# One transfer of an adaptive-norm transformer block's modulation matrix, split by partitions

## The chip, the cores and the metric

The kernel runs on one core of one Trainium2 chip. The metric is the device time of one execution in microseconds (us); lower is better. A core has five engines with instruction streams of their own: TensorE (PE: matmuls, with weight loads shown as PEld), VectorE (DVE), ScalarE (ACT), GpSimd (POOL) and SyncE (SP), which here issues DMA transfers only. The transfers of SP and ACT run on the core's 16 DMA engines.

## The reference

One transformer block over 2048 tokens of width 640, in bf16. A vector c gives six modulation vectors of 640, which scale, shift and gate two sub-blocks: attention with 32 heads of 20 over a causal window of 256 tokens, and a gated feed-forward of width 1536.

```python
mod = (silu(c) @ w_mod).reshape(1, 6, 1, -1)          # w_mod: 640 x 3840
sa, ca, ga, sb, cb, gb = (mod[:, i] for i in range(6))
h = layernorm(x) * (1 + ca) + sa
x = x + ga * attention(h, A_wqkv, A_wo)               # 0 <= query - key < 256
h = layernorm(x) * (1 + cb) + sb
x = x + gb * ((sigmoid(h @ w_gate) * (h @ w_up)) @ w_down)
```

## The kernel before

Tokens are worked in eight chunks of 256, each two blocks of 128 rows. A chunk goes through layer norm, transposes, the modulation, the q, k and v projections, windowed attention, the output projection, the second layer norm and the feed-forward; work of neighbouring chunks is interleaved.

The program is first written as a list of operations (`A(...)`, in the class `Prog`), each with its engines, what it reads and writes, and an assumed cost. The order in which they are issued is written out by hand in the list `PLAN` (L365): each code is five times an operation's number plus the number of its engine (0 TensorE, 1 ScalarE, 2 VectorE, 3 GpSimd, 4 SyncE). `emit` (L262) turns the dependencies into semaphore waits. Every engine works its instructions strictly in that order, so an instruction that waits holds up all behind it on its engine. Transfers take one of 24 semaphores in turn (`NDMA`, L25), and a transfer whose semaphore was used before waits for the transfer that used it.

The beginning is what the change touches. `load_bulk` (L621) loads a weight matrix in pieces of row blocks. For the first modulation matrix, `wm0` (the columns of w_mod for sa and ca, 640 x 1280), it makes five transfers, one for each block of 128 rows: 128 partitions of 2560 bytes, 320 KB (KiB). They go into the memory that later holds wd, so the profile names them wd<-in_w_mod_dram; all transfers show line L584. They are operations 18 to 22, and the plan has them on SP in the order of blocks 1, 0, 3, 2, 4 (codes 99, 94, 109, 104, 114). Ahead of them stand c, a part of wq (240 KB) and two blocks of x (160 KB each, one issued by SP, one by ACT); behind them on SP the rest of wq, two more blocks of x, and wk, wo and wv.

TensorE meanwhile runs matmuls on zeros (L679), then transposes the normalized first x block. For each block of wm0 it then has ten matmuls (`fnA`, L768) that add silu(c) times that block into the bank psA, with filling matmuls on zeros (L690) between some, and the transposes of the second x block between blocks 1 and 2. VectorE copies the sum into mA (L778); with mA, ScalarE, VectorE and GpSimd modulate the transposed x, hT (L831, L832), and the first projections (wq, hT) follow.

Of the kernel before, what the change touches and what calls it, by code (L numbers as in the profile page):

```python
# [360 lines left out]
def c_pe(n):  # L361
# [129 lines left out]
MW = 64  # L491
# [14 lines left out]
def build(nc, A_x, A_wqkv, A_wo, B_x, B_w_gate, B_w_up, B_w_down, c, w_mod, out, S=2048):  # L506
    NCH = S // CH
    P = Prog(nc)
    A = P.op
# [55 lines left out]
    def R(name):  # L565
        return Res(name)

    R_w3 = {k: [R(k + "0"), R(k + "1")] for k in ("wq", "wk", "wv")}
    R_crow, R_ident, R_ccol, R_cth, R_siluc, R_silubc = (R(n) for n in ("crow", "ident", "ccol", "cth", "siluc", "silubc"))
# [45 lines left out]
    Rm = [[R(f"wm{i}_{kt}") for kt in range(NDT)] for i in range(4)]  # L615
# [149 lines left out]
    oA = []  # L765
# [622 lines left out]
```

## Time and profile before

| | us |
|---|---|
| median of three runs | 324.57 |
| the three runs | 322.55, 324.57, 632.56 |
| the profiled execution, whole | 323.56 |
| its span, first to last instruction | 321.8 |
| TensorE busy in the span | 315.6 (98%) |

The profile is of one execution. A busy time sums what an engine's instructions cover; matmuls are pipelined and overlap, so a covered stretch need not be work at full speed. "L698 PE MATMUL S<-silubc,wd" is line, engine, operation, and the tile written and those read; "x10" is how many. A bracket such as [0.50 <-DVE x L815] gives the idle time of the engine ahead of the row, and what ended it. Rows of SPq and ACTq are transfers being issued; from issue to landing is told by another view. The chain of work that ended last is followed back from the last instruction to what released each. In the view by stages, each engine's busy time (and instructions) stands in the order PE, PEld, DVE, ACT, POOL, then TensorE's granted clock, the share in which the 16 DMA engines were busy, and GB/s.

### The profile page before, as it was taken

How to read it: one execution, taken by the hardware profiler on the slowest of the kernel's cores; microseconds unless marked ns; L12 is line 12 of the kernel's file. 1: busy time of each engine (PE TensorE's matmuls, PEld its weight loads, DVE VectorE, ACT ScalarE, POOL GpSimd, SP SyncE). 2: the span in 40 equal slices, each digit the busy share in tenths (PEclk: the TensorE clock that was granted, in tenths of full speed). 3: DMA queues.
4: the chain of work that ended last, by engine and by line, in shares of the span. 5: the costliest groups of instructions: out<-in, count | busy, mean ns of one | idle time of the engine just before them, and what ended most of it. 6: DMA issues, size and time to landing. Idle time of an engine off the chain costs nothing.

```text
span 321.8 us, 11465 instructions
## 1 busy us (share of the span) xinstructions
PE 315.6 (98%) x5045; PEld 236.8 (74%) x5045; DVE 198.8 (62%) x424; ACT 213.9 (66%) x229; POOL 189.5 (59%) x349
## 2 busy tenths in 40 slices
PE   6999999999999999999999999999999999999996
PEld 2677767677877777766777677877877777877885
DVE  4689987877886746584555555465534474386323
ACT  2699997877787986768686867676976746411220
POOL 3338759878768493949484848577575826601000
PEclk9999999999999999999999999999999999999999
DMA  7999999999922534126526100220800004002101
GB/s 249 348 262 278 223 179 248 194 225 295 206 36 43 88 75 55 44 63 108 77 19 111 37 22 2 63 42 25 132 18 4 22 22 104 20 5 61 43 0 41
DMA packets 62123, 32.92 MB, mean 102 GB/s; under 512 B 45946, under 2 KB 60794, under 8 KB 62074
## 3 DMA queue, kind: packets, MB, share of 16 engines
q1 hardware_dynamic: 59904, 29.73, 43.5%
q10 hardware_dynamic: 2170, 2.46, 2.8%
q8 instruction: 39, 0.64, 0.9%
q14 instruction: 10, 0.08, 0.1%
HBM read 18.68 MB, written 2.62 MB: 66 GB/s over the span
## 4 chain that ended last, share of the span: by engine, by line
PE 96%; DMA 1%; DVE 1%; ACT 1%; issue 0%; ACTq 0%
PE M L698 79%; PE S L699 8%; PE M L699 7%; DMA x<-in_A_x_dram 1%; ACT hT L831 1%; DVE st L793 1%; PE S L698 1%; PE S L690 0%; ACT stg L914 0%; ACTq L584 0%; DVE x L815 0%; DVE st L795 0%; ACT hT L914 0%; DVE x L1308 0%; DVE mA L778 0%
## 5 line engine op out<-in xcount | busy, mean ns | idle before, releaser
L1067 ACT ACTIVATE E<-S 128x2048 bf16<-128x2048 f32 x56 | 105.0, 1875 | 40.6 <-PE S L699 40.2
L1072 POOL TENSOR_SCALAR_AFFINE_SELECT E<-E 128x256 bf16<-128x256 bf16 x112 | 46.6, 427 | 57.1 <-ACT E L1067 25.1
L1076 POOL TENSOR_SCALAR_AFFINE_SELECT E<-E 128x512 bf16<-128x512 bf16 x112 | 70.6, 646 | 4.6 <-DVE x L815 1.2
L698 PE MATMUL M<-h2T,wg 128*128 128x256 bf16 x480 | 67.0, 273 | 0.0
L698 PE MATMUL M<-h2T,wu 128*128 128x256 bf16 x480 | 66.7, 273 | 0.0
L1289 DVE SCALAR_TENSOR_TENSOR hh<-sig,M 128x512 bf16<-128x512 f32 x48 | 32.4, 678 | 42.9 <-ACT sig L1287 26.4
L698 PE MATMUL M<-wd,hh 128*128 128x320 bf16 (+2 forms) x396 | 57.1, 295 | 0.0
L698 PEld LDWEIGHTS M<-h2T,wg 128*128 128x128 bf16 x480 | 45.4, 98 | 7.8 <-DVE T L1162 0.2
L698 PEld LDWEIGHTS M<-h2T,wu 128*128 128x128 bf16 x480 | 45.2, 98 | 7.3
L1287 ACT ACTIVATE sig<-M 128x512 f32<-128x512 f32 x48 | 28.5, 595 | 31.2 <-PE M L698 30.9
L698 PEld LDWEIGHTS M<-wd,hh 128*128 128x128 bf16 x396 | 37.2, 98 | 13.7 <-DVE hh L1289 0.2
L1045 POOL TENSOR_SCALAR_AFFINE_SELECT E<-E 128x1024 bf16<-128x1024 bf16 x28 | 32.0, 1147 | 4.9 <-ACT E L1041 3.4
L699 PEld LDWEIGHTS S<-QT,KT 20*64 20x64 bf16 (+1 forms) x1856 | 20.0, 100 | 17.4 <-issue 9.7
L699 PE MATMUL S<-QT,KT 20*64 20x256 bf16 (+5 forms) x1856 | 32.3, 228 | 0.4 <-issue 0.4
L1041 ACT ACTIVATE E<-S 128x2048 bf16<-128x2048 f32 x14 | 26.3, 1876 | 6.8 <-PE S L699 6.7
L793 DVE BATCH_NORM_STATS2 st<-x 128x6 f32<-128x320 bf16 x64 | 28.9, 479 | 2.4 <-DMA x<-in_A_x_dram 1.8
L1162 DVE STREAM_TRANSPOSE T<-M 128x512 f32<-128x512 f32 x32 | 21.5, 700 | 12.9 <-PE S L699 11.6
L698 PE MATMUL M<-wk,hT 128*128 128x320 bf16 x160 | 27.9, 299 | 0.0
L1308 DVE TENSOR_TENSOR x<-M,x 128x320 bf16<-128x320 f32 (+2 forms) x33 | 15.4, 475 | 18.8 <-PE M L698 18.6
L698 PE MATMUL M<-wq,hT 128*128 128x320 bf16 x160 | 26.2, 299 | 0.7 <-DVE hT L832 0.5
L698 PE MATMUL M<-wv,hT 128*128 128x320 bf16 x160 | 26.0, 299 | 0.0
L698 PE MATMUL M<-wo,oT 128*128 128x320 bf16 x160 | 25.9, 299 | 0.0
(84 smaller groups left out, 356.4 us busy)
## 6 DMA issues: line engine op xcount, KB each, us to landing
x<-in_A_x_dram SPq DMA_DIRECT2D x18, 160.0 KB, 3.7
wd<-in_w_mod_dram SPq DMA_DIRECT2D x6, 320.0 KB, 5.4
wd<-in_B_w_down_dram SPq DMA_DIRECT2D x4, 480.0 KB, 5.5
wu<-in_w_mod_dram SPq DMA_DIRECT2D x5, 320.0 KB, 4.8
x<-in_A_x_dram ACTq DMA_DIRECT2D x8, 160.0 KB, 2.7
out_dram<-x SPq DMA_DIRECT2D x8, 160.0 KB, 1.9
wu<-in_B_w_up_dram SPq DMA_DIRECT2D x2, 576.0 KB, 4.7
wg<-in_B_w_gate_dram SPq DMA_DIRECT2D x2, 576.0 KB, 6.8
```

The source lines that it names most:

```text
L698: return e.matmul(o, l, r, start=st, stop=sp, skip_group_check=True)
L699: return e.matmul(o, l, r, start=st, stop=sp, tile_position=tp, skip_group_check=True)
L793: A("dve", lambda e, g, bi=bi, j=j: e.bn_stats(v(bi * 12 + j * 6, 6), src[bi].ap[:, j * 320:(j + 1) * 320]), 0.48, reads=[src[bi].r()], wr ...
L1041: A("act", lambda e, eng: e.activation(cell().rearrange("p m (x c) -> p m x c", c=64)[:, :, 0:4:3, :], Sp.ap[:].rearrange("p j (k x c) -> ...
L1045: A("pool", lambda e, eng, c0=c0, pat=pat, base=base, cm=cm: e.affine_select(cell()[:, :, c0:c0 + 64], cell()[:, :, c0:c0 + 64], pattern=p ...
L1067: A("act", lambda e, eng: e.activation(part(0, 512), Sp.ap[:], ACT.Exp, scale=SM_SCALE), 1.876, reads=[Sp.r()], writes=[E.r("C"), E.r("B") ...
L1072: A("pool", lambda e, eng, hc=hc, src=src, far_h=far_h: e.affine_select(side(hc), part(src, 64), pattern=[[0, 4], [-1 if far_h else 1, 64] ...
L1076: A("pool", lambda e, eng, c0=c0, near=near: e.affine_select(part(c0, 128), part(c0, 128), pattern=[[0, 4], [1 if near else -1, 128]], com ...
L1162: A("dve", lambda e, g, h=h: e.transpose(T1.ap[:, 512 * h:512 * h + 512], X[h].ap), 0.694, reads=[X[h].r()], writes=[T1.r(h)], prio=3.5, t ...
L1287: A("act", lambda e, g, pg=pg, sg=sg: e.activation(sg.ap[:], pg.ap[:], ACT.Tanh, scale=0.5), c_act(512), reads=[pg.r()], writes=[sg.r()], ...
L1289: A("dve", lambda e, g, pu=pu, sg=sg, f0=f0: e.scalar_tensor_tensor(out=hh.ap[:, f0:f0 + 2, :], in0=sg.ap[:].rearrange("p (a b) -> p a b", ...
L1308: A("dve", lambda e, g, ps=ps, bi=bi, c0=c0, n=n: e.tensor_tensor(x1[bi].ap[:, c0:c0 + n], ps.ap[:, 0:n], x1[bi].ap[:, c0:c0 + n], op=ALU. ...
```

## The change

The transfer of block 0 of wm0 becomes two, one for partitions 0 to 119 and one for partitions 120 to 127. They are issued by SP one right behind the other, at the old one's place. The second has a result of its own, `R_wm0x`, and the ten matmuls of block 0 wait for both. Since there is one operation more, every operation from number 19 on has its number raised by one, and with it its code in the plan; apart from the added code 99 behind 94 the plan's order is the same.

```diff
 PLAN = [
-    119, 53, 76, 3, 8, 297, 86, 84, 300, 305, 333, 270, 277, 99, 281, 48, 442, 335, 28, 437, 447, 94, 13, 287, 422, 427,
...
+    124, 53, 76, 3, 8, 302, 86, 84, 305, 310, 338, 275, 282, 104, 286, 48, 447, 340, 28, 442, 452, 94, 99, 13, 292, 427,
...
     def load_bulk(dst, src, Rs, work, prio, tag, extra=(), cuts=(1, 2, 3, 4, 5), dlat=2.24):
         k = 0
         for m in cuts:
+            if tag == "wm0" and k == 0:
+                dma(lambda: dst[0:120, 0:1, :], lambda: src[0:120, 0:1, :], 0.8, writes=Rs[0:1], prio=prio, tag=tag, dlat=dlat, tmin=0.44, lat=0.18)
+                dma(lambda: dst[120:128, 0:1, :], lambda: src[120:128, 0:1, :], 0.08, writes=[R_wm0x], prio=prio, tag=tag, dlat=dlat, tmin=0.44, lat=0.18)
+                k = m
+                continue
...
+    R_wm0x = R("wm0x")
     load_bulk(wm_ap[0], wm_src[:, :, 0:1280], Rm[0], 0.88, 0.2, "wm0", dlat=2.89)
...
-        oA.append(A("pe", fnA, MW / 2400.0 * 10, reads=[Rm[0][kt], R_silubc], writes=[psA.r()], prio=0, lat=0.2, tag="modA"))
+        oA.append(A("pe", fnA, MW / 2400.0 * 10, reads=[Rm[0][kt], R_silubc] + ([R_wm0x] if kt == 0 else []), writes=[psA.r()], prio=0, lat=0.2, tag="modA"))
```

218 rows, old and new, of the table PLAN are left out of this document.

## The prediction

> **What bounds the kernel now.** I read the busy shares first, then the same shares by stage, then the chain that ended last.
>
> ```profile
> span 321.8 us, 11465 instructions
> PE 315.6 (98%) x5045; PEld 236.8 (74%) x5045; DVE 198.8 (62%) x424; ACT 213.9 (66%) x229; POOL 189.5 (59%) x349
> ...
> 0.00:14.00 14.00, 10.54 (x94) 5.42 (x95) 6.62 (x23) 5.61 (x12) 5.28 (x24) 1.00 0.91 292
> 14.00:282.00 268.00, 267.60 (x4632) 200.76 (x4631) 172.90 (x365) 201.73 (x206) 182.21 (x321) 1.00 0.50 103
> ```
>
> TensorE (PE) is busy for 315.6 of 321.8 us. By stage it is busy for 267.60 of 268.00 us between 14 and 282 us, but for only 10.54 of the first 14 us; the changed transfer lies in those. The DMA engines are 0.91 busy there and 0.50 later. So the program is a crowded head, then a solid run of TensorE work in a fixed order. What the head gains or loses shifts that run one for one; what arrives earlier behind the head finds TensorE busy anyway.
>
> The chain in order of time shows what holds the head. Columns are start, length, what:
>
> ```profile
> 1.40 3.38 DMA x<-in_A_x_dram
> ...
> 9.82 0.98 PE S L698 x30
> 10.80 0.02 issue
> 10.83 0.18 DVE mA L778
> 11.00 0.03 issue
> 11.03 0.88 ACT hT L831 x2
> ...
> 13.19 0.65 ACT stg L914 x2
> 13.85 0.09 issue
> 13.94 4.24 PE M L698 x43
> ```
>
> A block of x lands at 4.78 us, is normalized, and at 9.82 the chain is on the modulation matmuls ("PE S L698"). At 10.83 VectorE copies their result (mA), ScalarE modulates hT, and from 13.94 TensorE runs solid. No modulation transfer stands in this chain by name, but the view credits pipelined TensorE work with all time it covers, so a short stall inside "x30" would not show. I look for it in the next two views.
>
> TensorE's own rows, start and length, weight loads as PEld:
>
> ```profile
> 7.47 0.45 PE L698 MATMUL M<-ident,x 128*128 128x128 bf16 x5 [1.50 <-DVE x L815]
> 7.47 0.28 PEld L698 LDWEIGHTS M<-ident,x 128*128 128x128 bf16 x5 [1.99 <-DVE x L815]
> 7.80 0.47 PE L698 MATMUL S<-silubc,wd 128*128 128x64 bf16 x10
> 8.32 0.45 PE L698 MATMUL S<-silubc,wd 128*128 128x64 bf16 x10
> 8.61 0.38 PE L690 MATMUL S<-E 128*128 128x512 bf16 x1
> 8.93 0.11 PEld L698 LDWEIGHTS M<-ident,x 128*128 128x128 bf16 x2 [0.25 <-DVE x L815]
> 9.06 0.59 PE L690 MATMUL S<-E 128*128 128x512 bf16 x2
> 9.66 1.13 PE L698 MATMUL S<-silubc,wd 128*128 128x64 bf16 x30
> L698 PE MATMUL S<-silubc,wd x50: 192/193/203, 7.8 to 10.6; 128*128 128x64 bf16 x50
> ```
>
> The ten matmuls at 7.80 are row block 0 of the matrix, those at 8.32 block 1, the thirty at 9.66 blocks 2, 3 and 4. One takes 0.193 us and they overlap. At 8.32 the last of ten starts at 8.32 + 0.45 - 0.193 = 8.58, so starts are 0.257 / 9 = 0.0286 us apart. At 9.66 the last of thirty starts at 9.66 + 1.13 - 0.193 = 10.60, 0.94 after the first, where 29 steps of 0.0286 make 0.83. So **0.11 us** of stall lies within the thirty.
>
> The issues and landings of the five transfers, each from a window over one issue (last column: us from issue to landing):
>
> ```profile
> 1.82 2.34 SPq L584 DMA_DIRECT2D wd<-in_w_mod_dram x5
> wd<-in_w_mod_dram SPq DMA_DIRECT2D x1, 320.0 KB, 5.1
> wd<-in_w_mod_dram SPq DMA_DIRECT2D x1, 320.0 KB, 5.4
> wd<-in_w_mod_dram SPq DMA_DIRECT2D x1, 320.0 KB, 5.8
> wd<-in_w_mod_dram SPq DMA_DIRECT2D x1, 320.0 KB, 6.5
> ```
>
> Five issues in 2.34 us are 0.47 apart: at 1.82, 2.29, 2.76, 3.23 and 3.70. The written order sends blocks 1, 0, 3, 2, 4 (code 99 stands ahead of 94 in the plan), so the changed "first" transfer, block 0, is the second issue. The four rows are issues one, two, three and five; the fourth has none. Block 1 lands at 6.9, block 0 at 2.29 + 5.4 = 7.7, block 3 at 8.6, block 4 at 3.70 + 6.5 = 10.2. Blocks 2 and 3 would be done at 9.66 + 20 x 0.0286 = 10.23, and a landing has to pass to TensorE: block 4 is the only one that arrives as late as it is needed, and I put the 0.11 us down to it. Block 0 also arrives (7.7) just as TensorE is ready for it (7.80).
>
> **Why a landing can move at all.** The DMA share and rate of the head:
>
> ```profile
> 0.00:2.00 2.00, 0.69 (x2) 0.28 (x3) 0.33 (x1) 0.20 (x1) 1.28 (x9) 1.00 0.02 4
> 2.00:4.00 2.00, 2.00 (x7) 0.62 (x6) 0.17 (x1) 1.29 (x2) 0.50 (x6) 1.00 0.96 288
> 4.00:6.00 2.00, 1.98 (x7) 0.56 (x5) 1.15 (x5) 0.00 (x0) 0.00 (x0) 1.00 0.99 325
> 6.00:8.00 2.00, 0.53 (x12) 0.48 (x13) 1.59 (x5) 0.47 (x1) 1.23 (x4) 1.00 1.03 376
> 8.00:10.00 2.00, 2.00 (x41) 1.39 (x37) 0.93 (x3) 0.53 (x2) 0.94 (x4) 1.00 1.09 366
> ```
>
> Summing rate by time, 584 KB (thousands of bytes) were moved by 4.0 us, 1234 by 6.0, 1986 by 8.0. Up to and with both x blocks, 240 + 1.2 + 2 x 160 KiB = 575 KB were queued, reached at 4.0; x landed at 4.78, so 0.8 later. With blocks 1 and 0 it is 1230 KB, reached at 6.0; block 0 landed 1.7 later. With all five it is 2213 KB, reached at 8.0 + 227 / 366 = 8.6; block 4 landed 1.6 later. So from x to block 0 the last part falls another 0.8 us behind the mean, and stays there. That is what one late engine of the sixteen would look like, since a transfer is complete only with its slowest share. One engine moves 376 / 16 = 23.5 GB/s; its eight rows of 2560 bytes in a transfer take 0.87 us, one row 0.11. An engine left out of one transfer makes up just what the late one lacks.
>
> **The change part by part.**
>
> *The 120-row transfer.* If 8 rows each go to 15 engines, those take as long as before and the sixteenth gains 0.87 us for all later blocks. Bounds for block 0's landing: not before 6.0 + 0.8 = 6.8, not after today's 7.7 plus one row. Bounds for block 4: 10.2 - 0.87 = 9.3 if the late engine is the one relieved, 10.3 if it is another. I take the first, since the lag is one engine's share in size.
>
> [...] No view here shows engine numbers. [...]
>
> *The 8-row transfer.* One more issue on SP, 0.47 us by the row of five. Everything behind it on SP (blocks 3, 2, 4, then the rest of wq, x, wk, wo, wv) is issued 0.47 later. Block 4 then goes out at 4.2 and is still queued for about 4 us, since the engines never drain (share 0.96 to 1.09): this costs nothing while they are full. Later SP has a spare wait, given below, that takes it up. On the engines the eight rows cost nothing in bytes; those that carry one row more are 0.11 us later, and 9.3 to 9.6 for block 4 remains ahead of 10.2.
>
> *The added wait.* Block 0's matmuls now wait for two landings. Queued behind them on TensorE are fills, block 1 and the transposes of the second x. The small piece is issued at 2.76 and stands right behind its sister; I take 6.9 and the upper bound is the next transfer's 8.6. At 6.9 it is hidden: TensorE has loaded the weights of the five transposes ahead of block 0 only at 7.47 + 0.28 = 7.75. The wait instruction itself costs between nothing and 0.09 us (the "issue" pieces of the chain are 0.02 to 0.09), and is covered: a fill holds up the next matmul for 0.59 - 0.38 = 0.21 us (two at 9.06), so the fill of 8.61 is through at 8.82, and TensorE waits until 8.93 for VectorE. The same gap swallows any earlier start of block 0.
>
> *The counters.* Transfers take 24 counters in turn; the 25th waits for the first. With one more, that becomes the wo transfer at 14.57, waiting for a transfer landed 2.7 us after issue. No cost. Pairs later on are as before.
>
> ```profile
> 14.57 0.44 SPq L584 DMA_DIRECT2D wo<-in_A_wo_dram  x1
> DMA to landing us min/median/max: 2.7/6.9/7.2
> SPq L584 <- PE M L698: 3.7, 1, 3.7
> ```
>
> The last row is the spare wait: SP idles 3.7 us for TensorE soon after the head.
>
> *Sum.* The 0.11 us stall before block 4 goes; what is late next is TensorE itself, which then has blocks 2, 3, 4 back to back, so no more than 0.11 can be had. mA moves from 10.83 to 10.72, the ScalarE chain and the solid run with it. The profiled execution took 323.56 us around its span of 321.8: 323.56 - 0.11 = **323.45**. The undisturbed runs shown are 322.55 and 324.57, whose mean is 323.56 too, so I keep that base and not the listed median of 324.57. A measurement of this kernel tells about 2% (6.5 us) from no change, and runs differ by 2 us: the expected gain is far below both.
>
> **The rivals.**
>
> *Nothing moves.* If the late engine still carries its rows, or the lag isn't one engine's, block 4 lands at 10.2 to 10.3 and the time is 323.56 to 323.67. For it: no view names the engine. Against it: the lag of 0.8 us appears once and then stays, as a single early delay would. [...]
>
> *The small piece is late.* If it lands like a transfer of its own behind the next, at 8.6 in place of 7.7, block 0's matmuls start 0.8 us later than 7.80; 0.11 of it is slack before 8.93, and mA comes some 0.7 later with a stall gone: 324.2. It decides once the piece is later than about 7.9. Against it: it queues ahead of block 3.
>
> *Few engines (the other side).* If the 120 rows run on one engine, they take 120 x 0.11 = 13 us after x, landing near 18; block 0's matmuls slip from 7.80 to 18 and all behind them: about 333.7, 3% slower. It takes hold when the landing is past 7.75 and passes 2% at 14.3, so only one engine would do it; two (6.6 us, landing near 11.5) cost 3.7. Against it: nothing in the trace speaks for such a spread, and 128 rows at 0.87 us a transfer plainly use all.
>
> *More than the stall.* The second x pair and wq also land up to 0.87 us earlier. VectorE waits there, and ScalarE's chain might shorten too: at most the 0.52 us of that wait, 322.9.
>
> ```profile
> 12.31 1.50 DVE L793 BATCH_NORM_STATS2 st<-x 128x6 f32<-128x320 bf16 x3 [0.52 <-DMA x<-in_A_x_dram]
> ```
>
> Against it: TensorE is solid when that work is wanted.
>
> **How the numbers follow.** Forecast 0.66, nothing moves 0.18, more than the stall 0.06, late piece 0.07, few engines 0.03. The unknown costs span 322.9 to 324.2; runs of one kernel lie about 1 us to either side of their mean, so the range is 321.8 to 325.2. Faster by over 2% has no case but a misjudged head, 0.01; slower by over 2% is the few-engine case, 0.03; the rest, 0.96, is within.
>
> **What would show it.** Right: block 0's large part lands near 6.9, block 4 near 9.4 to 9.6; "x30" shrinks from 1.13 to 1.02; mA starts near 10.72 and the solid run near 13.83; six issues of wd on SP in 2.8 us. Wrong: landings of block 4 still 10.2 or later, a gap of TensorE ahead of its first ten modulation matmuls, or a chain through that transfer. The forecast fails outright if those matmuls start past 8 us.

## The result and the profile after

The changed kernel is slower, by a little: a median of 325.39 us (22 executions) against 323.69 us for the kernel before (22 executions; the 324.57 above was of the first three). The ratio is 1.0051 with a 95% interval of 1.0034 to 1.0069, some 1.65 us. One of the 22 executions of the kernel before took 632.56 us, and the ratio leaves it out. The change is within 2%, but clear of noise and on the wrong side of the forecast. The profiled execution took 325.89 us, its span is 324.2 us, 2.4 more than before.

The chain of the changed kernel, at the places where I showed it before:

```profile
2.79 0.04 issue
2.84 5.91 DMA wd<-in_w_mod_dram
8.75 0.14 issue
8.88 0.45 PE S L704 x10
...
12.09 1.20 PE S L704 x30
13.29 0.02 issue
13.31 0.18 DVE mA L784
13.49 0.02 issue
13.52 0.88 ACT hT L837 x2
...
15.68 0.65 ACT stg L920 x2
16.33 0.08 issue
16.41 4.24 PE M L704 x43
```

It no longer begins with x. A transfer of the modulation matrix, the 8-row one issued at 2.84, lands at 8.75, and all waits for it: mA starts at 13.31 in place of 10.83 (2.48 later), and the solid run at 16.41 in place of 13.94 (2.47 later). The end is 2.4 later. In this execution the head's loss went through one for one, as the prediction said a gain would.

TensorE's rows in the head of the changed kernel (start, length):

```profile
6.88 0.45 PE L704 MATMUL M<-ident,x 128*128 128x128 bf16 x5 [0.57 <-DVE x L821]
8.88 0.45 PE L704 MATMUL S<-silubc,wd 128*128 128x64 bf16 x10 [1.55 <-DMA wd<-in_w_mod_dram]
9.17 0.57 PE L696 MATMUL S<-E 128*128 128x512 bf16 x1
9.54 0.74 PE L704 MATMUL S<-silubc,wd 128*128 128x64 bf16 x10
11.88 1.39 PE L704 MATMUL S<-silubc,wd 128*128 128x64 bf16 x30
```

The x transposes come even earlier than before (6.88 against 7.47; x happened to land early in this execution), but then TensorE stands idle for 1.55 us, and block 0's matmuls start 1.08 later than the 7.80 of before. From there to mA takes 13.31 - 8.88 = 4.43 us, where it took 10.83 - 7.80 = 3.03. So the 2.48 us are two losses: **1.08 of waiting and 1.40 of slower work**. Each has its row. First the transfers, by stretch; the columns of the 2.00 us are TensorE busy, granted clock, DMA share and GB/s. The kernel before:

```profile
5.50:7.50 2.00, 0.51 (x4) 1.00 1.02 370
6.00:9.00 3.00, 1.52 (x28) 1.00 1.03 374
9.20:12.40 3.20, 2.71 (x44) 1.00 1.12 370
```

The changed kernel:

```profile
5.50:7.50 2.00, 1.26 (x8) 1.00 1.04 238
6.00:9.00 3.00, 0.88 (x12) 1.00 1.02 291
9.20:12.40 3.20, 3.20 (x34) 0.50 1.10 364
```

While the 120 rows are moved, the DMA engines are as busy as ever (1.04 against 1.02) but move **238 in place of 370 GB/s**. By the packets counted in the 2.00 us, one took 0.15 us of an engine on average (216 in 103.9% of the time of 16 engines), where it had taken 0.10 (325 in 102.3%). And from 9.2 to 12.4 the granted TensorE clock is **0.50**; ahead of it TensorE had been busy for only 0.88 of 3 us, against 1.52. The issues and landings, again from windows over one issue, for the 120 rows and for block 4:

```profile
wd<-in_w_mod_dram SPq DMA_DIRECT2D x1, 300.0 KB, 6.2
wd<-in_w_mod_dram SPq DMA_DIRECT2D x1, 320.0 KB, 6.9
```

The 120 rows, issued at 2.31 as before, land at 8.5 (block 0 landed at 7.7), and block 4 at 4.0 + 6.9 = 10.9 in place of 10.2.

### The profile page after: what moved, and what is told of

Same layout as the page of the kernel before. It is cut to its first block, busy times and chain, and to the rows that moved or that the text cites. A ratio compares the mean times of both kernels' runs of the same rounds, so it can differ in the third digit from the quotient of the medians.

```text
span 324.2 us, 11466 instructions
## 1 busy us (share of the span) xinstructions
PE 317.4 (98%) x5045; PEld 237.9 (73%) x5045; DVE 198.4 (61%) x424; ACT 213.8 (66%) x229; POOL 188.9 (58%) x349
## 4 chain that ended last, share of the span: by engine, by line
PE 95%; DMA 2%; ACT 1%; SPq 1%; issue 0%; DVE 0%
PE M L704 79%; PE S L705 8%; PE M L705 7%; DMA wd<-in_w_mod_dram 2%; PE S L704 1%; SPq L584 1%; ACT hT L837 1%; PE S L696 1%; ACT stg L920 0%; ACT hT L920 0%; DVE x L1314 0%; DVE mA L784 0%
```

## The experiments

**Theory:** the transfer of 120 partitions is itself slow, by its shape (238 GB/s, where 128 partitions had 370 in the same stretch); the rest follows from block 0 being late. **Rivals:** one more transfer and one more wait cost this; the 8-row piece lands late of itself; 120 is a bad count because 16 does not divide it; the slow side is the reading. All kernels are compared with the kernel before on the same chip.

### Two transfers, cut by columns

```diff
-  dst[0:120, 0:1, :]   and  dst[120:128, 0:1, :]
+  dst[:, 0:1, 0:640]   and  dst[:, 0:1, 640:1280]
```

> Block 0 again as two transfers with two waits, but cut by columns: 128 partitions of 1280 bytes each, in place of 120 and 8 partitions. [...] Rival (one transfer more, one wait more is what costs): block 0 lands near 8.7 as in the changed kernel, TensorE stands idle ahead of its matmuls, 1 to 2.5 us slower.

Ratio 0.9996 (0.9976 to 1.0016): no difference. From this run's stages and its VectorE rows:

```profile
5.50:7.50 2.00, 1.64 (x10) 1.00 0.98 346
10.29 0.17 DVE L784 COPY mA<-S 128x10 f32<-128x10 f32 x1 [1.37 <-PE S L704]
```

The rate is 346 GB/s. Block 0's matmuls start at 7.46 without waiting for a transfer, so both parts land by then, ahead of the 7.6 to 8.0 that I expected if it is the 120 rows that are slow, and mA starts at 10.29, ahead of the 11 that I expected. One more issue, one more wait and two landings cost nothing that these runs can show (0.5 us at most, by the interval). That rival is out.

### Two transfers of 64 partitions

```diff
-  dst[0:120, 0:1, :]  and  dst[120:128, 0:1, :]
+  dst[0:64, 0:1, :]   and  dst[64:128, 0:1, :]
```

> Block 0 as two transfers of 64 partitions each (0 to 63, 64 to 127). [...] Rival that it is the odd count (120 does not divide by 16 engines): 64 does, so the rate stays and block 0 lands by 8.0, within 0.6 us of the kernel before.

Ratio 1.0031 (1.0010 to 1.0052), median 324.76 against 323.56: slower by 1.0 us by the interval's middle, the low end of the 1 to 2.5 us that I expected if any run of partitions shorter than 128 is slow.

```profile
5.50:7.50 2.00, 0.45 (x6) 1.00 1.06 241
2.92 5.28 DMA wd<-in_w_mod_dram
```

The rate is 241 GB/s, as in the changed kernel; the second row is of this run's chain, where the second half, issued at 2.92, lands at 8.20. That is sooner than the 8.6 to 9 that I expected. 64 divides by 16, so a low rate doesn't need the odd count.

### 128 partitions, and 8 rows once more

The first transfer is whole again; rows 120 to 127 are loaded a second time, into memory that nothing uses yet (`wd_flat` is short for wd with the columns of a partition in one row), and block 0's matmuls wait for both.

```diff
-  dst[0:120, 0:1, :]      and  dst[120:128, 0:1, :]
+  dst[:, 0:1, :]          and  wd_flat[120:128, 6400:7680]
```

> Block 0 as one transfer of 128 partitions, and rows 120 to 127 loaded a second time as a transfer of 8 partitions into unused memory, with the wait for both. Theory (the 120-row part is slow): the extra transfer costs one row on its engines, 0.1 to 0.2 us; block 0 lands by 8.1; within 0.6 us of before. Rival (the small transfer itself lands late or holds up the queue): the landing and the time are those of the changed kernel, 1 to 2.5 us slower.

Ratio 1.0010 (0.9993 to 1.0028), median 323.64: as the theory expected. The profiled execution (325.37 us) is one of the two of 12 above 325; in it block 0 lands at 8.13 (8.1 was expected) and the clock falls, which I take up below.

```profile
5.50:7.50 2.00, 0.87 (x7) 1.00 0.95 338
2.31 5.82 DMA wd<-in_w_mod_dram
```

### The small piece first

The changed kernel with code 99 (the 8 rows) moved ahead of blocks 1 and 0 in the plan.

```diff
- ... 282, 104, 286, ... 452, 94, 99, 13, ...
+ ... 282, 99, 104, 286, ... 452, 94, 13, ...
```

> The changed kernel with the 8-row transfer issued ahead of blocks 1 and 0, so that it cannot be what block 0 waits for. Theory (the 120-row part is slow): the 120 rows still land near 8.5, and the time stays 1 to 2.5 us above the kernel before. Rival (the small piece arrives late): the wait goes, 323.5 to 324.

Ratio 1.0065 (1.0040 to 1.0090), median 325.48 against 323.56: no better than the changed kernel.

```profile
5.50:7.50 2.00, 0.24 (x5) 1.00 1.07 288
2.65 6.04 DMA wd<-in_w_mod_dram
11.55 0.17 DVE L784 COPY mA<-S 128x10 f32<-128x10 f32 x1 [2.37 <-PE S L704]
```

The chain now goes through the 120 rows, issued at 2.65 and landed at 8.69. The rate is low again, though less so than in the changed kernel's profile. So the small piece at 8.75 in the changed kernel was only the last to arrive behind its slow sister; as a cause of its own it is out.

### All five blocks split

```diff
-  if tag == "wm0" and k == 0:   # block 0 alone
+  if tag == "wm0":              # 120 and 8 partitions for every block
```

> All five blocks split into 120 and 8 partitions. Theory (each 120-row transfer takes its packets at half rate, some 0.7 us more for each): block 4 lands 3 to 4 us later than in the kernel before, near 13.5, packets of 2560 bytes average near 0.2 us through the five, and the time is 3 to 6 us above before. Rival (a single delay at the first of the transfers, whatever their number): block 4 lands near 11, 1.5 to 2.5 us above before.

Ratio 1.0100 (1.0069 to 1.0131), median 327.01 against 323.40: 3.6 us by the medians, within the expected 3 to 6.

```profile
5.00:11.00 6.00, 3.02 (x38) 1.00 1.04 248
5.21 7.45 DMA wd<-in_w_mod_dram
13.29 0.17 DVE L762 COPY mA<-S 128x10 f32<-128x10 f32 x1 [4.38 <-PE S L682]
```

The low rate now lasts for six microseconds, and the last landing is 12.66, 2.4 us behind the 10.2 of before, where I expected 3 to 4: 0.5 us for each block, not 0.7. It grows with the number of split blocks, as the theory wants. The clock stayed up in this profile and in two more of the four executions; the fourth, with the lower clock, was the fastest (326.81), so the clock has no visible part in this loss.

Over the kernels with block 0 whole or cut into 120 and 8, the rates fall into two groups. Between 5.5 and 7.5 us, those that load block 0 as 128 rows moved 338 to 370 GB/s (before 370, by columns 346, 8 rows once more 338, and two kernels below 352 and 348); the others, with 120 rows, moved 238 to 288 (changed 238, small piece first 288, all five split 249, the two with fills below 259 and 254). Each is one profile.

### Which side: the same 64 rows, written to two places

Block 0 is one transfer of 128 again. Behind it stands an extra transfer of rows 0 to 63 into memory that nothing uses yet; the two kernels differ only in the partitions written.

```diff
+  e10:  wd_flat[0:64,  6400:7680]  <-  src[0:64, 0, :]
+  e11:  wd_flat[32:96, 6400:7680]  <-  src[0:64, 0, :]
```

> Block 0 as one transfer of 128 partitions as in the kernel before, and one extra transfer of 64 rows (0 to 63 of the same block) into unused memory at partitions 0 to 63, with the wait for both. [...] Rival (the slow side is the reading, or the row count): the same as the next run.

> The same extra transfer, same 64 rows read, but written to partitions 32 to 95. [...] Rival (reading or row count): 230 to 300 GB/s here too, no difference between the two.

Written to partitions 0 to 63: median 327.42, ratio 1.0123 (1.0100 to 1.0147), and

```profile
5.50:7.50 2.00, 0.99 (x8) 1.00 1.01 294
wd<-in_w_mod_dram SPq DMA_DIRECT2D x1, 160.0 KB, 6.6
13.60 0.17 DVE L784 COPY mA<-S 128x10 f32<-128x10 f32 x1 [4.58 <-PE S L704]
```

Written to partitions 32 to 95: median 323.75, ratio 1.0005 (0.9985 to 1.0025), and

```profile
5.50:7.50 2.00, 1.28 (x13) 1.00 1.00 376
wd<-in_w_mod_dram SPq DMA_DIRECT2D x1, 160.0 KB, 4.5
10.87 0.17 DVE L784 COPY mA<-S 128x10 f32<-128x10 f32 x1 [2.00 <-PE S L704]
```

The same rows, read from the same place, take 6.6 us from issue to landing in one case and 4.5 in the other, and the stretch runs at 294 and at 376 GB/s. **For these 64 rows the partitions written decide**; that any run of partitions shorter than 128 is slow, which I tried with 64 and 64, is not so: 32 to 95 is one too. The difference in time, 3.7 us by the medians, is far above the 0.2 to 0.8 that I expected if the partitions written decide. In the first kernel's profile mA is 2.7 later, with the low clock on top of the late landing. But the clock doesn't account for all of it: of its four executions one has a granted clock of 1.0 and takes 327.38 us all the same. Why is open.

For 120 partitions no run separates the writing from the count of rows: the stretch ran at 238 GB/s with 0 to 119 in the changed kernel's profile, at 370 with 0 to 127 in that of before. No view shows which engine writes which rows. That the partitions written decide there too is my guess from this pair, not shown.

### Lateness alone

The kernel before, all transfers unchanged, where block 0's matmuls also wait for block 3.

```diff
-  reads=[Rm[0][kt], R_silubc]
+  reads=[Rm[0][kt], R_silubc] + ([Rm[0][3]] if kt == 0 else [])
```

> The kernel before, all transfers as they were, but the ten matmuls of block 0 also wait for block 3, which lands some 0.8 us after block 0. This makes lateness alone, with no slow transfer. Theory (the loss is the idle TensorE ahead of block 0, first by the lateness itself, then by a halved clock in some executions because TensorE was idle too long): block 0's matmuls start near 8.6, the time is 0.6 to 1.7 us above the kernel before, and some executions show a granted clock under 1. Rival (lateness up to 8.6 is hidden, the loss of the changed kernel has another source): within 0.3 us of before.

Ratio 1.0020 (0.9994 to 1.0046), median 324.12 against 323.40: the expected size, but the interval includes no change. In the profiled execution (clock 1.0) the matmuls start at 8.32, not the expected 8.6, and mA at 11.12, 0.3 late:

```profile
8.32 0.45 PE L698 MATMUL S<-silubc,wd 128*128 128x64 bf16 x10 [0.85 <-DMA wd<-in_w_mod_dram]
11.12 0.17 DVE L778 COPY mA<-S 128x10 f32<-128x10 f32 x1 [2.21 <-PE S L698]
```

The average hides two groups, which the granted clock over the span tells apart. The same division for the kernels that bear on it, which ran on different chips (executions, mean us):

| kernel | clock 0.999 or 1.0 | clock 0.995 |
|---|---|---|
| before (beside the first four experiments) | 30: 323.63 | 1: 325.24 |
| changed | 12: 324.54 | 10: 326.21 |
| block 0 waits for block 3 | 8: 323.78 | 4: 325.88 |
| changed, with fills (below) | 10: 324.86 | 1: 327.59 |

In the profiles with a clock of 0.995 it is one stretch at half speed near the start, in the changed kernel's at 0.50 from 9.22 to 12.64 us:

```profile
5.81:9.22 3.41, 1.29 (x19) 1.00 1.02 292
9.22:12.64 3.42, 3.42 (x37) 0.50 1.11 366
```

Half of 3.42 us is 0.5% of the span, which gives the 0.995. What the stretch costs can be read from the time between block 0's first matmul and mA: 11.12 - 8.32 = 2.80 us here at full clock, and 11.55 - 8.74 = 2.81 in the kernel with the small piece first, also at full clock; but 4.43 in the changed kernel and 12.62 - 8.18 = 4.44 in that with 8 rows once more, both with a half-clock stretch. So it costs 1.6 us in the head.

In this kernel 4 of 12 executions have the low clock and take 2.1 us more; the other 8 are as fast as before (323.78 against 323.76 beside them), where none of 23 executions of the kernel before has it. So a start up to 8.3, as profiled, is nearly free by itself; what goes with the loss is the low clock, which 4 of 12 executions have once block 0's matmuls wait (in the profile TensorE is idle for 0.85 us ahead of them).

### Fills in the idle time

A first attempt (e6) put seven filling matmuls behind the wrong group of transposes: they ran at 10.67, behind block 1's matmuls, and only added work.

> The changed kernel with seven more filling matmuls on zeros (some 1.5 us) between the first x transposes and block 0's matmuls, so that TensorE is not idle while it waits. Theory (part of the loss is the halved clock after that idle time): the granted clock stays 1.0 in all executions, block 0 still lands near 8.5, and the time is 0.4 to 1.2 us above the kernel before, in place of 1.8. Rival (the clock has no part in it): still 1.5 to 2 us above.

It took 327.01 us (1.0097, 1.0064 to 1.0129), with clock 0.995 in 3 of 6: it tells nothing of the question. The second stands in the gap itself:

```diff
   # behind the x transposes that come ahead of block 0's matmuls
+  for _ in range(7):
+      e.matmul(p_S.aps[0][:, 3, :], Eall[:, 0:128], Eall[:, 128:640], start=True, stop=True)
```

> The changed kernel with seven filling matmuls on zeros (some 1.5 us), this time right behind the two groups of x transposes that come ahead of block 0's matmuls. Theory (the loss has two parts: block 0 late by the slow 120-row transfer, worth 0.9 us in the executions whose clock stays at 1.0, and 1.7 us more in the 10 of 22 executions whose clock is halved for one stretch after the idle time): no execution shows a clock of 0.995, block 0's matmuls start at 8.6 to 9.0, and the time is 0.5 to 1.3 us above the kernel before. Rival (the low clock is not due to the idle TensorE): 0.995 appears in 3 to 6 of 10 executions and the time is 1.5 to 2 us above.

```profile
7.29 1.67 PE L862 MATMUL S<-E 128*128 128x512 bf16 x7
8.80 0.46 PE L704 MATMUL S<-silubc,wd 128*128 128x64 bf16 x10
```

The low clock is down to 1 execution of 11 from 10 of 22, where the theory expected none and the rival 3 to 6 of 10. That supports the idle time ahead of block 0's matmuls (1.55 us in the changed kernel's profile, none here) as its cause, without excluding chance altogether. The time is a miss: the ratio is 1.0051 (1.0030 to 1.0071), 1.65 us above the kernel before, in the rival's range and not in the theory's; its median is 324.79 against the changed kernel's 325.39, on another chip. This run doesn't tell what lateness costs at full clock (324.86 here, 324.54 in the changed kernel), because the fills got in the way themselves. In its profile the 120 rows, issued at 2.3, land 5.7 later, at 8.0:

```profile
wd<-in_w_mod_dram SPq DMA_DIRECT2D x1, 300.0 KB, 5.7
7.45 1.51 PE S L862 x7
```

The second row is of its chain, which goes through the fills until 8.96 and not through a transfer: the start at 8.80 is theirs.

The 3.41 us ahead of the half-clock stretch above were not idle throughout: TensorE was busy for 1.29 of them, and for 1.62 in the kernel with 8 rows once more. In the kernel with all five blocks split it was busy for 1.59 of the 3.41 us from 4.54 to 7.95, and the clock stayed up. How little work is too little, and why only some executions are hit, these runs don't settle.

### A try for a faster head

Not about the split: the first part of wq (240 KB) moved from the front of SP's queue to behind block 4.

```diff
-    119, 53, 76, ... 495, 114, 480, ...
+    53, 76, ... 495, 114, 119, 480, ...
```

> The kernel before with one thing moved: the first part of wq (240 KB), now the first transfer on SP, is issued behind block 4. Not about the split: if the landing of the modulation blocks (and of x) holds the head, as the theory has it, x and all five blocks land 0.5 to 0.8 us earlier, mA comes 0.3 to 0.8 us earlier, and the kernel is that much faster than before. Rival (the head is held by TensorE and by wq itself): no change, or slower by what wq is late for the first projection.

Ratio 1.0037 (1.0014 to 1.0059): slower. In its profile x lands at 4.92 and mA starts at 10.87, neither earlier than before (4.78 and 10.83). Block 1 is now issued ahead of that x block, at 1.25, which may be what holds x up. None of the versions beats the kernel before.

## Why the prediction was wrong

*What bounds the kernel.* Right: the head decides, and in the changed kernel's profile its shift goes through whole (2.48 at mA, 2.4 at the end). The stall inside "x30" was read rightly too: where nothing is late, as in the two-by-columns kernel, the thirty take 1.04 us, not 1.13, so 0.09 was all that could be had.

*"If 8 rows each go to 15 engines, those take as long as before."* **This step failed.** The prediction priced a row by the rate of 128-partition transfers and moved it to another shape. In that shape the engines moved 238 GB/s while fully busy (1.04), where the 128 rows had moved 370; the 120 rows landed at 8.5 and the small piece at 8.75, beyond the bounds of 6.8 to 7.8 set from that rate. The matmuls started at 8.88 behind a gap of 1.55 us, with the chain through that transfer: the signs that the prediction named for being wrong. That 120 rows go to 15 engines, eight to each, which the 0.87 us of gain and with it the 0.11 us of the sum stand on, no run shows; in its place the runs showed the lower rate. The two kernels that write the same 64 rows to different partitions show that such a change of rate can come from where the rows go (294 against 376 GB/s); that it is so for 120 no run shows. The prediction's nearest rows were all of 128 partitions, and its bound had no room for a lower rate.

*The late engine.* That one engine falls behind may hold for the execution shown; no view names it, and the landing it was read from moves by itself. In the two-by-columns kernel x landed at 4.35 where the profile before had 4.78, with no engine relieved:

```profile
1.41 2.94 DMA x<-in_A_x_dram
```

So a gain of 0.11 us from relieving one engine was built on one execution. With the rate down, any such gain could not be seen.

*The 8-row transfer.* An extra issue and an extra wait at no cost: right, shown by the kernels cut by columns (0.9996) and with 8 rows once more (1.0010). "I take 6.9" for its landing was wrong, with its sister.

*The added wait and TensorE's slack.* The price of lateness was given in the rival "the small piece is late": 0.8 later, 324.2. The changed kernel's executions at full clock average 324.54, 0.9 above the kernel before, so that rival came nearest, by another cause than its own. With the small piece first, at full clock, the profile has block 0's matmuls at 8.74 and mA at 11.55, 0.72 late: the rival's 0.7. What neither it nor any rival contained is the **clock**: 10 of 22 executions lose 1.7 us more (326.21 against 324.54). 0.9 + 10 / 22 x 1.7 = 1.7 us, the measured difference. The profile showed a clock of 1.00 throughout, and all that hinted at it was the 1.5 us in which TensorE already stood idle ahead of 7.47.

*The rest.* Of the 0.9 us at full clock not all is settled. In the 64 and 64 kernel's profile mA is 0.3 late, yet the span is 0.9 longer; between 40 and 64 us its TensorE is busy for 23.02 of 24 us against 23.60 before. Why some executions lose there is open. The first row is of the kernel before, the second of 64 and 64:

```profile
40.00:64.00 24.00, 23.60 (x382) 1.00 1.11 207
```

```profile
40.00:64.00 24.00, 23.02 (x396) 1.00 1.11 204
```

## What to carry to other kernels

Here a transfer's rate went with its shape: the same stretch ran at 370 GB/s with 128 partitions and at 238 with 120. So when a change cuts the partition count, don't take the rate measured on 128 partitions for a bound; and which partitions were written cost a fifth of the bandwidth (294 against 376 GB/s) with the engines as busy (1.01 and 1.00). Where a wait falls on a TensorE that is already half idle (busy for 1.52 of the 3 us from 6 to 9 in the kernel before), price the clock too: here the lateness cost 0.9 us at full clock, and the halved clock 1.7 us more in 10 of 22 executions. If a transfer has to be divided, try a cut by columns first; here it cost nothing measurable (0.9996), where both cuts by partitions did (1.0051 and 1.0031).

## What was not expected of the hardware

An extra 160 KB in the most crowded stretch cost nothing measurable when it was written to partitions 32 to 95 (1.0005), and 1.2% when the same rows went to 0 to 63. And in the changed kernel's profile, behind 1.55 us in which TensorE waited for block 0, the granted clock was 0.50 for 3.42 us; a mean clock of 0.995 stands in 10 of its 22 executions, against 2 of 83 of the kernel before over four chips.
